# Windowed attention and a two-layer FFN: the opening reordered, and weight pieces with other engines' instructions

## The chip, the cores and the metric

The kernel runs on one core of a Trainium2 chip. The metric is the device time of one execution in microseconds, shown as the median of several runs. TensorE (PE) does the matrix products, VectorE (DVE), ScalarE (ACT) and GpSimd (POOL) work on tiles, SyncE (SP) issues DMAs. SBUF holds the tiles, PSUM the products.

## The reference

Attention over a window of 64 positions, for batch 8, 8 heads, 576 positions and head size 64, then an FFN over 4608 tokens, 512 to 2048 to 512, with a mish activation:

```python
scores = scale * np.matmul(q, k.transpose(0, 1, 3, 2))
mask = (rel >= 0) & (rel < window)          # window = 64
scores = np.where(mask, scores, -1000000000.0)
attn = softmax(scores)
x = (attn @ v) as [4608, 512]
h = x @ w_in
sp = np.where(h > 20.0, h, np.log1p(np.exp(np.minimum(h, 20.0))))
g = h * np.tanh(sp)
out = (g @ w_out).astype(np.float32)
```

The softmax divides by its sum + 1e-9. q, k and v are float32; w_in and w_out arrive as float64.

## The kernel before

**Tiling.** The 4608 tokens form 12 chunks of 384. A chunk's attention is done for four pairs of heads (p = 0 to 3), each giving 128 of the 512 channels of x. Its FFN has 16 steps f, each over 128 of the 2048 hidden channels. A float32 product is made of three products of rounded parts: x is kept as xh + xl, the weights as high and low parts, the activation g as gh + gl.

**Attention of a pair** (`att_scores`, `att_transpose`, `att_values`). TensorE makes the scores (L126) in two PSUM tiles; VectorE adds the mask and finds the extreme, in six pieces (L135, two records each); ScalarE takes the exponential and its sum (L138); VectorE makes the reciprocal (L140, L141); GpSimd multiplies, six pieces (L143). Chunks 0 and 1 transpose with TensorE (L162) and copy by ScalarE (L163). Later chunks transpose 32x32 blocks on VectorE (L152) and move the blocks by twelve DMAs from SyncE (L157). TensorE multiplies with v (L177), and ScalarE and VectorE split the result into xh and xl (L179, L180). Tiles pr and tr share the tag "pr" with two buffers.

**An FFN step** is twelve products into h_ps (L188, `ffn_in`), a chain over ScalarE and VectorE (L195 to L205), gh and gl on GpSimd (L206, L207), and nine products into three accumulators (L218, `ffn_out`), which follow two steps later (LAG). h_ps has two buffers. With `alone`, h is first copied to SBUF (L199), so that h_ps comes free early.

**Weights.** There are 32 pieces of 128x512 words of 64 bits (`load_w`), one for w_in and one for w_out of each f. The first five are loaded by SyncE, the rest by GpSimd's queue. Integer operations build the float32 value: L243 or L245 drops the sign, L246 clamps, L248 to L250 shift and join, L251 (ScalarE) rounds to the high part, L252 subtracts for the low part: on VectorE for pieces 6 to 25, on GpSimd for the others. Buffers: st three, wa four (tag "t", shared with the FFN's t).

**Order of the opening.** The attention of chunks 0 and 1 comes first, eight pairs one after the other, with eight weight pieces held back until named points. Then come 24 FFN steps, (1,0), (0,0), (1,1), (0,1) and so on, with two pieces each, which finish chunk 1 and half of chunk 0, with `alone`. Then chunk 0's steps 8 to 15 run, with chunk 2's attention between them, and from there every chunk's 16 steps with the next chunk's attention between them.

**What sets the order.** Each engine runs its instructions in one fixed order. It comes from the order of the code and from a scheduler that may move an instruction ahead of others on its engine. The PSUM banks: three tiles "acc" for a chunk's accumulators, two for h_ps, three "at" for attention and for the accumulators of chunk 1. In the first two chunks the even pairs' attention uses the "acc" banks.

Of the kernel before, what the change touches and what calls it, by code (L numbers as in the profile page):

```python
# [27 lines left out]
def tile_window_attn_mish_ffn(  # L28
# [83 lines left out]
    def att_scores(c, p, tiles):  # L112
        q_t, k_t = tiles

        if c < 2 and p % 2 == 0:
# [13 lines left out]
        for m in range(NM):  # L129
            first = [(c * NB + 2 * m + par) % blocks_per_seq == 0 for par in range(2)]  # L130
            mk = firsts[first.index(True)] if any(first) else mask
            for h in range(2):
# [2 lines left out]
                marks[c, p] = nc.vector.tensor_tensor_reduce(  # L135
# [5 lines left out]
        nc.vector.reciprocal(sm, sm)  # L141
        for j in range(HM):
            nc.gpsimd.tensor_scalar(pr[:, j, :], pr[:, j, :], sm[:, j:j + 1], 0.0, ALU.mult, ALU.add)  # L143
# [23 lines left out]
    def att_values(c, p, v_t, pT, x):
        xh, xl = x
        if c < 2 and p % 2 == 0:
            o_ps = ps_acc.tile([P, CH], F32, name="o_ps", tag="acc2")  # L170
        else:
            o_ps = ps_at.tile([P, CH], F32, name="o_ps", tag="at")
# [9 lines left out]
    def ffn_in(x, f, alone=False):  # L182
# [17 lines left out]
        nc.vector.tensor_scalar(t, t, EXP20, 1.0, ALU.min, ALU.add)  # L200
# [210 lines left out]
```

## Time and profile before

| | us |
|---|---|
| median of 3 runs (lowest, highest) | 1050.46 (1048.21, 1053.51) |
| the profiled execution | 1050.85 |
| its span in the profile | 1049.1 |
| TensorE busy | 963.9 (92%) |
| VectorE, ScalarE, GpSimd busy | 460.3, 600.4, 444.4 |
| TensorE waiting for gh (L206) | 23.6 |

A row of the timeline has the start and the length in us, the engine, line, operation, tiles written and read, the shape and a count (a matmul record counts twice where the product is taken in two passes); in brackets stands the idle time before it and what ended it. Lengths of neighbours overlap by under 0.1 us, so that the distance of two starts is the true cost of a busy engine. A row of the windows has the stretch, its length, then busy us and count for PE, weight loads, DVE, ACT and POOL, then TensorE's granted clock, the DMA share and GB/s. Rows of groups end with busy us, mean ns, and the idle time before. A row of the page on DMAs ends with KB of one and us from issue to landing.

### The profile page before, as it was taken

To read this page: it belongs to the slowest core of one execution; us is meant where nothing else is said; L and a number is where in the kernel's file an instruction comes from. 1 tells how busy PE (TensorE), PEld (TensorE's weight loads), DVE (VectorE), ACT (ScalarE), POOL (GpSimd) and SP (SyncE) were. 2 spreads that over 40 slices of the span, in tenths; PEclk is the share of its full clock that TensorE was granted. 3 is DMA by queue.
4 is the path that set the end of the run, shared out by engine and by line. 5 is a ranking of instruction groups with operands and counts; after the bars stand their busy time and mean duration, and the time that the engine had idled before them with its cause. 6 is when DMAs were issued, how large, how long until landed. Compare 5 with 4: busy or idle time off the path is not lost.

```text
span 1049.1 us, 18496 instructions
## 1 busy us (share of the span) xinstructions
PE 963.9 (92%) x6384; PEld 825.5 (79%) x6384; DVE 460.3 (44%) x1317; ACT 600.4 (57%) x1524; POOL 444.4 (42%) x729
## 2 busy tenths in 40 slices
PE   5577669996499999999999999999999999999997
PEld 4356558985388888888888888888888888888896
DVE  3679995333334334334343343344343443443232
ACT  4545666653356556565555565565665565655664
POOL 4445455342244344435344344444344444344332
PEclk9678999998599999999999999999999999999999
DMA  7544440013212222222222221221222221210000
GB/s 226 155 155 140 141 140 1 1 59 112 83 50 77 66 60 76 76 66 67 73 66 64 74 80 53 73 78 54 74 78 53 74 77 53 90 50 17 31 1 31
DMA packets 84957, 78.56 MB, mean 75 GB/s; under 512 B 11136, under 2 KB 76160, under 8 KB 84864
## 3 DMA queue, kind: packets, MB, share of 16 engines
q1 hardware_dynamic: 80976, 63.22, 20.4%
q0 software_dynamic: 3888, 14.16, 4.0%
q8 instruction: 51, 0.84, 0.3%
q14 instruction: 42, 0.34, 0.1%
HBM read 56.10 MB, written 9.44 MB: 62 GB/s over the span
## 4 chain that ended last, share of the span: by engine, by line
PE 81%; DVE 8%; DMA 3%; ACT 3%; issue 2%; SPq 2%; POOL 1%; ACTq 0%; DVEq 0%; POOLq 0%
PE h_ps L188 38%; PE acc L218 35%; PE o_ps L177 4%; PE s_ps L126 4%; DMA st<-w_out 1%; ACT pr L138 1%; DVE wa L249 1%; SPq L157 1%; DVE wa L250 1%; DVE wa L248 1%; DVE wa L246 1%; POOL pr L143 1%; DVE t L205 1%; DVE pr L135 1%; DVE tr L152 1%
## 5 line engine op out<-in xcount | busy, mean ns | idle before, releaser
L188 PE MATMUL h_ps<-xh,wi_h 128*128 128x384 f32 x768 | 267.5, 349 | 11.1 <-DVE t L205 5.1
L188 PE MATMUL h_ps<-xh,wi_l 128*128 128x384 f32 x768 | 265.3, 345 | 0.0
L188 PE MATMUL h_ps<-xl,wi_h 128*128 128x384 f32 x768 | 265.0, 345 | 0.0
L206 POOL TENSOR_SCALAR gh<-t 128x384 fp32r<-128x384 f32 x192 | 105.2, 548 | 373.4 <-DVE t L205 354.0
L218 PE MATMUL acc<-wo_h,gh 128*128 128x512 f32 x576 | 233.0, 404 | 23.6 <-POOL gh L206 23.6
L218 PE MATMUL acc<-wo_l,gh 128*128 128x512 f32 x576 | 231.2, 401 | 0.0
L207 POOL TENSOR_TENSOR gl<-t,gh 128x384 fp32r<-128x384 f32 x192 | 196.7, 1024 | 15.8
L218 PE MATMUL acc<-wo_h,gl 128*128 128x512 f32 x576 | 202.7, 396 | 0.0
L195 ACT ACTIVATE t<-h_ps 128x384 f32<-128x384 f32 x192 | 93.9, 489 | 188.5 <-PE h_ps L188 152.7
L200 DVE TENSOR_SCALAR t<-t 128x384 f32<-128x384 f32 x192 | 107.2, 558 | 161.9 <-ACT t L195 161.9
L188 PEld LDWEIGHTS h_ps<-xh,wi_h 128*128 128x128 f32 x768 | 147.0, 192 | 27.1 <-DVE t L205 7.4
L143 POOL TENSOR_SCALAR pr<-pr,sm 128x128 f32<-128x128 f32 x288 | 107.2, 391 | 144.0 <-DVE sm L141 130.3
L205 DVE SCALAR_TENSOR_TENSOR t<-t,h_ps 128x384 f32<-128x384 f32 x152 | 83.5, 549 | 185.8 <-ACT t L203 185.6
L138 ACT ACTIVATE pr<-pr,mx 128x128 f32<-128x128 f32 x288 | 111.8, 390 | 85.6 <-DVE mx L135 85.6
L201 ACT ACTIVATE t<-t 128x384 f32<-128x384 f32 x192 | 100.6, 524 | 99.0 <-DVE t L200 98.4
L188 PEld LDWEIGHTS h_ps<-xl,wi_h 128*128 128x128 f32 x768 | 147.3, 192 | 8.9
L188 PEld LDWEIGHTS h_ps<-xh,wi_l 128*128 128x128 f32 x768 | 147.2, 192 | 2.7 <-issue 2.1
L218 PEld LDWEIGHTS acc<-wo_h,gh 128*128 128x128 f32 x576 | 109.6, 190 | 47.6 <-POOL gh L206 27.9
L218 PEld LDWEIGHTS acc<-wo_h,gl 128*128 128x128 f32 x576 | 107.8, 187 | 25.1 <-issue 0.5
L218 PEld LDWEIGHTS acc<-wo_l,gh 128*128 128x128 f32 x576 | 109.6, 190 | 17.5
L202 ACT ACTIVATE t<-t,half_b 128x384 f32<-128x384 f32 x192 | 118.3, 616 | 5.3
L203 ACT ACTIVATE t<-t 128x384 f32<-128x384 f32 x192 | 100.6, 524 | 5.2
(47 smaller groups left out, 719.1 us busy)
## 6 DMA issues: line engine op xcount, KB each, us to landing
v_t<-vN SPq DMA_DIRECT2D x48, 384.0 KB, 3.5
pT<-tr SPq DMA_DIRECT2D x480, 24.0 KB, 1.8
k_t<-kT SPq DMA_DIRECT2D x47, 224.0 KB, 2.7
out<-o SPq DMA_DIRECT2D x36, 256.0 KB, 2.1
q_t<-qT SPq DMA_DIRECT2D x47, 192.0 KB, 2.4
st<-w_out POOLq DMA_DIRECT2D x14, 512.0 KB, 3.7
st<-w_in POOLq DMA_DIRECT2D x13, 512.0 KB, 3.8
st<-w_in SPq DMA_DIRECT2D x3, 512.0 KB, 6.4
```

Of the source, the lines that this page charges most:

```text
L138: nc.scalar.activation(pr[:, j, :], pr[:, j, :], AF.Exp, bias=mx[:, j:j + 1], scale=-1.0, accum_out=sm[:, j:j + 1])
L143: nc.gpsimd.tensor_scalar(pr[:, j, :], pr[:, j, :], sm[:, j:j + 1], 0.0, ALU.mult, ALU.add)
L188: nc.tensor.matmul(h_ps, w[:, f, cc, :], xx[:, cc, :], start=n == 0, stop=n == 3 * NC_ - 1)
L195: nc.scalar.activation(t, h_ps, AF.Exp)
L200: nc.vector.tensor_scalar(t, t, EXP20, 1.0, ALU.min, ALU.add)
L201: nc.scalar.activation(t, t, AF.Square)
L202: nc.scalar.activation(t, t, AF.Ln, bias=half_b, scale=0.5)
L203: nc.scalar.activation(t, t, AF.Exp, scale=-1.0)
L205: nc.vector.scalar_tensor_tensor(t, t, -1.0, h, ALU.add, ALU.mult)
L206: nc.gpsimd.tensor_scalar(gh, t, 1.0, 0.0, ALU.mult, ALU.add)
L207: nc.gpsimd.tensor_tensor(gl, t, gh.bitcast(F32), ALU.subtract)
L218: nc.tensor.matmul(acc[t], a[:, ts_], w[:, f, :], start=f == 0 and i == 0, stop=f == NF - 1 and i == 2)
```

## The change

**Order.** Chunk 0's attention stands alone at the start, with one weight piece after each pair's scores and three behind. Then come seven steps of chunk 0 (HEAD = 7) with chunk 1's attention between them, then chunk 0's steps 7 to 15 in turn with chunk 1's steps 0 to 8, then chunk 1's last seven steps with chunk 2's attention between them. Two pieces follow every step of chunk 0. All attention events stand in one list; loads of q, k and v run on from a chunk to the next.

**Banks.** Chunk 2's attention uses the three "acc" banks, which chunk 0 has left by then; chunk 1's uses "at".

**Weight pieces.** All are loaded by SyncE. L255 drops the sign on VectorE in every piece; the clamp and the last subtraction are on GpSimd in every piece (L256, L262).

**Attention.** Only chunk 0 transposes with TensorE, one of its two copies now on VectorE; chunk 1 takes the VectorE and DMA way. The six softmax pieces go by head. In chunk 0 sums and multiplies are taken per head, and four of six multiplies are on VectorE.

**FFN.** Only the last chunk copies h. The +1 moves from VectorE's min into Square's bias; in chunks 0 and 1 the min of odd steps is on GpSimd (L212).

```diff
+    def banks(c, p):
+        if c == 2 or (c == 0 and p % 2 == 0):
+            return [(ps_acc, "acc0"), (ps_acc, "acc1"), (ps_acc, "acc2")]
+        return [(ps_at, "at")] * 3
...
+            if c == 0:
+                nc.vector.tensor_scalar(sm[:, js], sm[:, js], 1e-9, None, ALU.add)
+                nc.vector.reciprocal(sm[:, js], sm[:, js])
+                for j in range(h * NM, (h + 1) * NM):
+                    if j % NM == 1:
+                        nc.gpsimd.tensor_scalar(pr[:, j, :], pr[:, j, :], sm[:, j:j + 1], 0.0, ALU.mult, ALU.add)
+                    else:
+                        nc.vector.tensor_scalar(pr[:, j, :], pr[:, j, :], sm[:, j:j + 1], None, ALU.mult)
...
-        if c >= 2:
+        if c > 0:
             tr = ap_.tile([P, P // 32, HM, 32], F32, name="tr", tag="pr", bufs=2)
...
-            nc.scalar.copy(pT[:, :, h * NM:(h + 1) * NM, :].rearrange("p r m i -> p m r i"),
-                           t_ps.rearrange("p m (r i) -> p m r i", i=32))
+            (nc.scalar.copy if h == 0 else nc.vector.tensor_copy)(
+                pT[:, :, h * NM:(h + 1) * NM, :].rearrange("p r m i -> p m r i"),
+                t_ps.rearrange("p m (r i) -> p m r i", i=32))
...
-        nc.vector.tensor_scalar(t, t, EXP20, 1.0, ALU.min, ALU.add)
-        nc.scalar.activation(t, t, AF.Square)
+        if c < 2 and f % 2:
+            nc.gpsimd.tensor_scalar(t, t, EXP20, 0.0, ALU.min, ALU.max)
+        else:
+            nc.vector.tensor_scalar(t, t, EXP20, None, ALU.min)
+        nc.scalar.activation(t, t, AF.Square, bias=one_b)
...
-        (nc.sync if i < 5 else nc.gpsimd).dma_start(st, src)
+        nc.sync.dma_start(st, src)
...
-        if 1 <= i < 14:
-            nc.vector.tensor_scalar(a, hi, 0x7FFFFFFF, None, ALU.bitwise_and)
-        else:
-            nc.scalar.activation(af, hi.bitcast(F32), AF.Abs)
-        nc.vector.tensor_scalar(af, af, BIG, TINY, ALU.min, ALU.max)
+        nc.vector.tensor_scalar(a, hi, 0x7FFFFFFF, None, ALU.bitwise_and)
+        nc.gpsimd.tensor_scalar(af, af, BIG, TINY, ALU.min, ALU.max)
...
-        (nc.gpsimd if i < 6 or i >= 26 else nc.vector).tensor_tensor(wl, af, wh.bitcast(F32), ALU.subtract)
+        nc.gpsimd.tensor_tensor(wl, af, wh.bitcast(F32), ALU.subtract)
...
-    both = [(1, f) for f in range(NF)]
-    for f in range(F2):
-        both.insert(2 * f + 1, (0, f))
-    segments = [(both, None, None), ([(0, f) for f in range(F2, NF)], 2, 1)]
...
+    HEAD = 7
+    steps = [(0, f) for f in range(HEAD)]
+    for f in range(HEAD, NF):
+        steps += [(0, f), (1, f - HEAD)]
+    third = 2 * len(steps) + 2
+    steps += [(1, f) for f in range(NF - HEAD, NF)]
+    starts = {c: 2 * len(steps) + 2 * NF * (c - 2) for c in range(2, NCHUNK)}
+    steps += [(c, f) for c in range(2, NCHUNK) for f in range(NF)]
...
+    atts[1].plan(0, 2 * HEAD / (NPAIR + 1))
+    atts[2].plan(third, (starts[2] - third) / (NPAIR + 1))
+    for c in range(3, NCHUNK):
+        atts[c].plan(starts[c - 1], (2 * NF - 2) / (NPAIR + 1))
```

What the order shows at three places.

VectorE in the middle of the opening, before (wa, st: a weight piece; wi_l, wo_l: its low part; t, h: the FFN step):

```order
L250 SCALAR_TENSOR_TENSOR wa_886<-st_884,wa_886 128x512
L205 SCALAR_TENSOR_TENSOR t_907<-t_907,h_911 128x384
L249 SCALAR_TENSOR_TENSOR wa_934<-st_932,wa_934 128x512
L246 TENSOR_SCALAR wa_944<-wa_944 128x512
L250 SCALAR_TENSOR_TENSOR wa_934<-st_932,wa_934 128x512
L252 TENSOR_TENSOR wo_l_105<-wa_886,wo_h_104 128x512
L248 TENSOR_SCALAR wa_944<-wa_944 128x512
L252 TENSOR_TENSOR wi_l_103<-wa_934,wi_h_102 128x512
```

The same engine in the change, at chunk 1's first steps:

```order
L255 TENSOR_SCALAR wa_1249<-st_1247 128x512
L255 TENSOR_SCALAR wa_1259<-st_1257 128x512
L214 TENSOR_SCALAR t_1194<-t_1194 128x384
L214 TENSOR_SCALAR t_1227<-t_1227 128x384
L258 TENSOR_SCALAR wa_1249<-wa_1249 128x512
L259 SCALAR_TENSOR_TENSOR wa_1249<-st_1247,wa_1249 128x512
L219 SCALAR_TENSOR_TENSOR t_1194<-t_1194,h_ps_1181 128x384
L260 SCALAR_TENSOR_TENSOR wa_1249<-st_1247,wa_1249 128x512
```

And GpSimd in the change, at the same place:

```order
L256 TENSOR_SCALAR wa_1249<-wa_1249 128x512
L256 TENSOR_SCALAR wa_1259<-wa_1259 128x512
L220 TENSOR_SCALAR gh_1195<-t_1194 128x384
L221 TENSOR_TENSOR gl_1196<-t_1194,gh_1195 128x384
L220 TENSOR_SCALAR gh_1228<-t_1227 128x384
L262 TENSOR_TENSOR wi_l_103<-wa_1249,wi_h_102 128x512
L221 TENSOR_TENSOR gl_1229<-t_1227,gh_1228 128x384
L262 TENSOR_TENSOR wo_l_105<-wa_1259,wo_h_104 128x512
```

The clamp and the subtraction have left VectorE's order; between L255 and L258 of a piece VectorE now waits for GpSimd.

TensorE in chunk 2's attention, before (s_ps: scores of the next pair; o_ps: values of the pair before, which need its DMAs into pT):

```order
L177 MATMUL o_ps<-pT_107,v_t 64x64 x2
L126 MATMUL s_ps<-k_t,q_t 64x128 x12
L177 MATMUL o_ps<-pT_107,v_t 64x64 x10
L188 MATMUL h_ps<-xh_1812,wi_h 128x384 x2
L188 MATMUL h_ps<-xl_1813,wi_h 128x384
L188 MATMUL h_ps<-xh_1812,wi_l 128x384
L188 MATMUL h_ps<-xl_1813,wi_h 128x384
L188 MATMUL h_ps<-xh_1812,wi_l 128x384
L177 MATMUL o_ps<-pT_106,v_t 64x64 x2
L126 MATMUL s_ps<-k_t,q_t 64x128 x12
```

And in the change, at the scores of pair 2:

```order
L234 MATMUL acc_1_1292<-wo_h,gl 128x512
L127 MATMUL s_ps<-k_t,q_t 64x128 x12
L234 MATMUL acc_2_1293<-wo_h,gh 128x512
L234 MATMUL acc_2_1293<-wo_l,gh 128x512
L188 MATMUL o_ps<-pT_106,v_t 64x64 x2
L234 MATMUL acc_2_1293<-wo_h,gl 128x512
L199 MATMUL h_ps<-xh_605,wi_h 128x384
```

The scores of pair 2 now stand ahead of the first values of the chunk, those of pair 0; before, each pair's scores stand behind the first two products of the pair before.

SyncE in the change, in chunk 1's attention (st: weights; pT: transposing DMAs):

```order
L249 DMA st_735<-w_in 128x512
L169 DMA pT0_106<-tr_591 32x192 x12
L104 DMA q_t_661<-qT 128x384
L106 DMA k_t_662<-kT 128x448
L249 DMA st_745<-w_out 128x512
L113 DMA v_t_622<-vN 128x6x128
L249 DMA st_846<-w_in 128x512
L249 DMA st_856<-w_out 128x512
L169 DMA pT1_107<-tr_721 32x192 x12
```

Before, no transposing DMA stands in the opening, and weights from the sixth piece on are not in this queue.

More of the change, by code (lines that the diff above doesn't have):

```diff
@@ L113, in att_scores @@
         q_t, k_t = tiles
-        if c < 2 and p % 2 == 0:
-            s_ps = [ps_acc.tile([P, NM, P], F32, name="s_ps", tag=f"acc{h}") for h in range(2)]
-        else:
-            s_ps = [ps_at.tile([P, NM, P], F32, name="s_ps", tag="at") for h in range(2)]
+        s_ps = [pool.tile([P, NM, P], F32, name="s_ps", tag=tag) for pool, tag in banks(c, p)[:2]]
         pr = ap_.tile([P, HM, P], F32, name="pr", bufs=2)
@@ L168, in att_values @@
         xh, xl = x
[L169 to L172, printed above, removed]
+        pool, tag = banks(c, p)[2]
+        o_ps = pool.tile([P, CH], F32, name="o_ps", tag=tag)
         for n in range(NB):
@@ L180, in att_values, with ffn_in @@
         nc.vector.tensor_tensor(xl[:, p, :], o_ps, xh[:, p, :].bitcast(F32), ALU.subtract)
-    def ffn_in(x, f, alone=False):
+    def ffn_in(c, x, f, alone=False):
         xh, xl = x
@@ L334, in flush @@
             ffn_store(c, accs.pop(c))
-    todo_w = [(w, f) for f in range(NF) for w in (load_w_in, load_w_out)]
+    todo_w = [(load_w_in, 0)]
+    for f in range(NF):
+        todo_w += [(load_w_in, f + 1)] * (f + 1 < NF) + [(load_w_out, f)]
     def take_w(n):
@@ L341, in take_w @@
             w(f)
-    xs = {}
-    first = [Att(c, c) for c in range(2)]
-    first[0].next = first[1]
-    ev = []
-    for u in range(2 * NPAIR):
-        a, p = first[u // NPAIR], u % NPAIR
-        ev += [(u, 2, a.scores, p), (u + 0.75, 1, a.transpose, p), (u + 1.25, 0, a.values, p)]
-    for _, _, fn, i in sorted(ev, key=lambda e: e[:2]):
-        fn(i)
-    xs[0], xs[1] = first[0].x, first[1].x
-    for u in (2, 4, 5, 5, 6, 7, 7, 7):
-        with tc.issue_after(marks[u // NPAIR, u % NPAIR].ins):
-            take_w(1)
@@ new lines, in tile_window_attn_mish_ffn @@
+    for f in range(HEAD, NF):
[4 more added lines that the diff above has]
+    steps += [(c, f) for c in range(2, NCHUNK) for f in range(NF)]
+    atts = [Att(c) for c in range(NCHUNK)]
+    for a, b in zip(atts, atts[1:]):
+        a.next = b
+    for p in range(2):
+        atts[0].load(p, "qk")
+        atts[0].load(p, "v")
+    ev = []
@@ L371, in tile_window_attn_mish_ffn @@
+    for n, (c, f) in enumerate(steps):
+        if f == 0:
+            while any(fn.__self__ is atts[c] for _, _, fn, _ in events):
+                run(events[0][0])
+        pend.append((c, f, ffn_in(c, atts[c].x, f, c == NCHUNK - 1)))
+        run(2 * n)
+        if len(pend) > LAG:
+            flush()
+        run(2 * n + 1)
+        if c == 0:
             take_w(2)
-        if att:
-            att.run(1e9)
     while pend:
```

99 lines of the change are left out of this document (40 added, 59 removed).

## The prediction

> **What bounds the kernel now.** I first read the page's slices, to see where TensorE is not busy, then windows of 25 us there, then the engines' timelines in those windows.
>
> ```profile
> span 1049.1 us, 18496 instructions
> PE   5577669996499999999999999999999999999997
> DVE  3679995333334334334343343344343443443232
> ```
>
> A slice is 26 us. From the seventh slice on TensorE is full but for the 10th and 11th (digits 6 and 4); what can be won lies there and in the first six slices.
>
> ```profile
> 75.00:100.00 25.00, 19.38 (x78) 16.41 (x79) 24.45 (x45) 13.27 (x27) 12.82 (x14) 0.86 0.36 113
> 125.00:150.00 25.00, 16.31 (x74) 13.54 (x73) 24.67 (x41) 16.70 (x31) 13.40 (x15) 0.97 0.49 164
> 175.00:200.00 25.00, 25.00 (x125) 22.40 (x124) 6.01 (x11) 13.30 (x27) 8.83 (x13) 1.00 0.00 1
> 250.00:275.00 25.00, 8.71 (x82) 6.76 (x82) 6.01 (x30) 5.69 (x26) 4.21 (x12) 0.56 0.40 120
> ```
>
> From 75 to 150 us VectorE (third figure) is busy 24.5 us of 25: the opening is bound by VectorE, which turns the weights' 64-bit words into two float parts. At 175 the weights are done and TensorE is full. At 250 nothing is busy: that is a wait, taken up below.
>
> **What VectorE really waits for.** Its busy time holds blocked time.
>
> ```profile
> 144.10 0.68 DVE L249 SCALAR_TENSOR_TENSOR wa<-st,wa 128x512 uint32<-128x512 uint32 x1
> 144.81 1.81 DVE L250 SCALAR_TENSOR_TENSOR wa<-st,wa 128x512 uint32<-128x512 uint32 x1
> 147.46 1.94 DVE L249 SCALAR_TENSOR_TENSOR wa<-st,wa 128x512 uint32<-128x512 uint32 x1
> ...
> 144.75 1.32 POOL L252 TENSOR_TENSOR wi_l<-wa,wi_h 128x512 fp32r<-128x512 f32 x1
> 147.56 1.28 POOL L252 TENSOR_TENSOR wo_l<-wa,wo_h 128x512 fp32r<-128x512 f32 x1
> ```
>
> The instruction that takes 0.68 us at 144.10 takes 1.81 and 1.94 us when GpSimd's 1.3 us subtraction runs beside it: it is lengthened by 1.13 and 1.26 us, nearly the subtraction's whole time. So work that leaves VectorE for GpSimd still holds VectorE up. How much of it, the rate tells:
>
> ```profile
> 78.73 0.69 DVE L250 SCALAR_TENSOR_TENSOR wa<-st,wa 128x512 uint32<-128x512 uint32 x1
> 102.95 0.35 DVE L200 TENSOR_SCALAR t<-t 128x384 f32<-128x384 f32 x1
> 103.22 0.42 DVE L246 TENSOR_SCALAR wa<-wa 128x512 f32<-128x512 f32 x1
> 103.56 0.68 DVE L250 SCALAR_TENSOR_TENSOR wa<-st,wa 128x512 uint32<-128x512 uint32 x1
> 104.16 0.42 DVE L248 TENSOR_SCALAR wa<-wa 128x512 uint32<-128x512 uint32 x1
> ...
> 119.67 0.55 DVE L205 SCALAR_TENSOR_TENSOR t<-t,h 128x384 f32<-128x384 f32 x1
> 120.14 0.69 DVE L252 TENSOR_TENSOR wo_l<-wa,wo_h 128x512 fp32r<-128x512 f32 x1
> ...
> 142.08 1.50 DVE L250 SCALAR_TENSOR_TENSOR wa<-st,wa 128x512 uint32<-128x512 uint32 x1
> ...
> 163.74 0.68 DVE L250 SCALAR_TENSOR_TENSOR wa<-st,wa 128x512 uint32<-128x512 uint32 x1
> ...
> 181.68 0.51 POOL L206 TENSOR_SCALAR gh<-t 128x384 fp32r<-128x384 f32 x1 [4.72 <-DVE t L205]
> 182.27 1.02 POOL L207 TENSOR_TENSOR gl<-t,gh 128x384 fp32r<-128x384 f32 x1
> ```
>
> From start to start, unblocked, VectorE needs 0.27 us for the 384-wide scalar op, 0.34 for a 512-wide one, 0.60 for a 512-wide two-input op, 0.47 for L205. L250 ends a piece. Between the rows at 78.73 and 142.08 lie 17 pieces and 9 FFN steps, 3.73 us a piece. VectorE's own work is 2x0.34 + 3x0.60 (+0.34 in a third of them, L243) = 2.6, and 9/17 x (0.27+0.47) = 0.4. The missing 0.73 x 17 = 12.4 us stand against 9 x (0.51+1.02) = 13.8 us of GpSimd: 90% of it shows as VectorE time. From 142.08 to 163.74 GpSimd does the subtraction, VectorE has four ops as in the changed kernel, and 5 pieces with two to three steps take 21.7 us: **4.33 us a piece, dearer than 3.73**.
>
> **The change, part by part.** (1) *Weight pieces.* All 32 now have four VectorE ops, 2x0.34 + 2x0.60 = 1.88 us, and on GpSimd a clamp and the 1.3 us subtraction. That is the form of the last five pieces plus the clamp. No row shows a 512-wide clamp on GpSimd; L206 gives 0.51 us at 384 columns, and L143 six ops of 128 in 2.11 us, 0.35 each:
>
> ```profile
> 252.91 2.11 POOL L143 TENSOR_SCALAR pr<-pr,sm 128x128 f32<-128x128 f32 x6 [7.42 <-DVE sm L141]
> 6.50 0.29 DVE L135 CUSTOM_DVE_ANT_0 pr<-s_ps,mask 128x128 f32<-128x128 f32 x1 [6.50 <-PE s_ps L126]
> 7.77 0.08 DVE L135 DVE_READ_ACCUMULATOR2_ANT mx<- 128x1 f32 x1
> 43.90 0.56 DVE L180 TENSOR_TENSOR xl<-o_ps,xh 128x384 fp32r<-128x384 f32 x1
> ...
> 70.91 0.69 PE L188 MATMUL h_ps<-xh,wi_h 128*128 128x384 f32 x1
> ```
>
> The line through both gives 0.6 us. Bounds of what it costs VectorE: 0 (hidden) and 0.8 (all of it, and two hand-overs between the engines); I take 0.4, nearer to the one-input gh, which blocks less than gl. A piece then costs 4.33 + 0.4 = 4.7 us with 0.45 steps in it, and a further step 1.9 us (0.14+0.47 on VectorE, the rest gh and gl at 90%).
>
> (2) *Stage A, chunk 0's attention alone.* VectorE has, up to the chunk's last xl, the ops of 7 pieces (14 us with the gaps between dependent ones), five sets of six reduces (1.3 us each by the rows at 6.50 and 7.77), and some 9 us of sums, reciprocals, half the multiplies, two-bank copies and xl: 29.5 us. GpSimd blocks it for seven clamps (2.8) and about four subtractions (5) and some multiplies (1). With the start at 6.5 us, x of chunk 0 is whole at **45 us**; now it is at 44.4 (the row at 43.90), but the FFN goes on to its first whole h_ps only at 70.91, after chunk 1's attention. Splitting each pair's multiplies over two engines shortens a chain of 2.1 us that VectorE's queue covers anyway: nothing.
>
> (3) *Stage B, eight steps of chunk 0 beside chunk 1's attention.* 14 pieces x 4.7 = 66; 8 steps where 6.3 are in that price, 3; three subtractions left from A, 4; four pairs at 3.7 us (1.3 reduces, 0.4 sums, 1.0 transposition, 0.5 xl, and a quarter of L143's 2.1), 15: **88 us**, to 133. TensorE needs 8 x 4.2 + 6 = 40 of it. SyncE now issues weights too, between the twelve transposing DMAs of a pair (7.9 us, row below); per pair that is about 11 us in 22, so it is hidden by VectorE; if VectorE took under 13 us a pair it would be bared.
>
> (4) *Stage C, both chunks in turn, until the last piece.* 11 x 4.7 + (10-5) x 1.9 = **61 us**, to 194. TensorE needs 42.
>
> (5) *The rest of the two chunks.* Unhindered, a step is 4.21 us:
>
> ```profile
> 195.05 2.09 PE acc L218 x9
> 197.14 2.12 PE h_ps L188 x12
> ```
>
> By TensorE's order nine groups of h_ps and ten of acc lie between the step of the last piece and the first scores of chunk 2; one of each should be done by then, as TensorE has slack: 8 x 2.12 + 9 x 2.09 = 36 us, to 230. At this point before (217.90) exactly as much FFN is left: five h_ps and seven acc groups.
>
> (6) *Chunk 2's attention.*
>
> ```profile
> 217.90 0.89 PE L126 MATMUL s_ps<-k_t,q_t 64*64 64x128 f32 x24
> 248.30 0.34 PE L177 MATMUL o_ps<-pT,v_t 128*64 128x64 f32 x4 [0.59 <-DMA pT<-tr]
> 248.56 0.89 PE L126 MATMUL s_ps<-k_t,q_t 64*64 64x128 f32 x24
> ...
> 274.98 0.48 PE L177 MATMUL o_ps<-pT,v_t 128*64 128x64 f32 x4 [5.97 <-DMA pT<-tr]
> ...
> 224.90 0.98 DVE L152 STREAM_TRANSPOSE tr<-pr 128x768 f32<-128x768 f32 x1 [2.01 <-POOL pr L143]
> 225.90 7.89 SPq L157 DMA_DIRECT2D pT<-tr  x12
> 282.25 1.13 ACT L195 ACTIVATE t<-h_ps 128x384 f32<-128x384 f32 x2 [1.74 <-PE h_ps L188]
> ...
> pT<-tr SPq DMA_DIRECT2D x480, 24.0 KB, 1.8
> ```
>
> Now each pair's scores stand behind the first o_ps of the pair before, which waits for its DMAs: 13.3 us a pair (248.30 to 274.98 are two), 64.4 us from 217.90 to the first whole h_ps of chunk 2 (282.25). In the new order the scores of pairs 1, 2 and 3 stand ahead of that, so softmax runs while the DMAs do. What is late next is the two buffers of tag pr: tr of a pair waits for the DMAs of the one before, 1.0 + 7.9 + 1.8 to land = 10.7 us. From scores to the first tr 7.0 (217.90 to 224.90), four times 10.7, then values, xh and h_ps 3: **53 us**, so chunk 2's first h_ps at 283. The freed banks themselves are never the last wait.
>
> (7) *From there* 1049.1 - 282.3 = 767 us with TensorE full and nothing moved. The min that lost its add keeps one VectorE op; Square takes the add at no row's cost. The ten later chunks are at nothing; if ScalarE's added bias operand cost 0.1 us it would still be hidden.
>
> **Sum**: 45 + 88 + 61 + 36 + 53 + 767 = 1050, against a span of 1049.1; the profiled execution took 1050.85 (1.75 around the span), 0.4 above the median of 1050.46. I forecast **1052 us**: opening gains paid back by GpSimd's blocking.
>
> The Trainium skill, page "SBUF — State Buffer", section "Who interferes with whom", says that the port pair shared by VectorE and GpSimd is an exclusive lock for a whole instruction. By it all of GpSimd's time, not 90%, counts against such VectorE ops, and 25 pieces would take some 5 us more: 1057, inside the forecast's own range. The trace agrees with a lock, at 90% (12.4 of 13.8 us).
>
> **Rivals.** *Ops that don't collide.* In the opening L205 now reads h from PSUM, not from a copy in SBUF.
>
> ```profile
> L205 DVE SCALAR_TENSOR_TENSOR t<-t,h 128x384 f32<-128x384 f32 x24 | 16.7, 697 | 16.7 <-ACT t L203 16.6
> L205 DVE SCALAR_TENSOR_TENSOR t<-t,h_ps 128x384 f32<-128x384 f32 x12 | 6.6, 547 | 12.0 <-ACT t L203 12.0
> ```
>
> The second form is never lengthened. If GpSimd works beside it, the reduces, xl and copies, and the clamp hides too, 18 x 0.47 + some 7 us of the rest + 25 x 0.4 = 26 us go: **1026**. The same page of the Trainium skill exempts a VectorE op with at most one SBUF input outside the two-port modes; 547 against 697 ns agrees. Against it: queues run in order, so VectorE seldom has such an op at the moment it is blocked.
>
> *Idle on top, slower.* A piece now goes VectorE, GpSimd, VectorE, and GpSimd's queue holds 2.1 us of L143 and 1.0 of gl ahead of clamps; in stage B the reduces of a pair wait for the pair before to land, 10.7 us after its transposition, with only 4 to 6 us of VectorE work in between. If each of 25 pieces waits 0.5 us more and each of four pairs 2 us, 20 us come on top: **1072**. It decides once VectorE stands idle over 10% of stages B and C.
>
> *Chunk 2's wait stays.* If the scores still run one pair at a time, 64 us instead of 53: **1063**. The order speaks against it.
>
> **Chances**: forecast 0.45 (its own range 1040 to 1062), no collision 0.28, idle 0.20, the wait stays 0.07. Range 1022 to 1077, the first and the last of these cases with the clamp's bounds. A measurement can tell about 0.5% (5 us): faster takes 0.28 and a quarter of the forecast's range, 0.38; slower 0.37; the same 0.25.
>
> **What would show it.** First h_ps of chunk 0 near 45 us; last L260 near 194; VectorE over 95% busy from 20 to 190 with L259 and L260 well above 0.8 us on average; chunk 2's first scores near 230 and first h_ps 53 us later; 767 us from there. A last L260 before 180 or after 205 makes the prediction wrong, and so would a last part other than 767.

## The result, and the profile after

The changed kernel takes **1020.83 us** (median of 4 runs, 1019.57 to 1021.59), the kernel before 1051.99 (4 runs, 1048.21 to 1054.14) on the same chip: ratio 0.971, with a 95% interval of 0.967 to 0.974. The profiled execution has a span of 1019.6 us against 1049.1. The forecast was 1052, with a range of 1022 to 1077: it was wrong, by 31 us at its centre.

The slices of the page of the changed kernel (span, TensorE and VectorE, 25.5 us each):

```profile
span 1019.6 us, 18461 instructions
PE   4677677998699999999999999999999999999998
DVE  5988767233333344444444444343344444444322
```

TensorE's low digits now lie in the first seven slices and in the 11th; the second dip of before (6 and 4, in the 10th and 11th) has become an 8 and a 6. VectorE's digits in the opening (second to seventh slice) are 6 to 9, lower than the forecast thought (over 95%).

The forecast named three places to look at. They stand in the timelines of VectorE (last weight piece), TensorE (first scores of chunk 2) and ScalarE (first whole h_ps of chunk 2); columns: start, duration, instruction.

```profile
178.72 1.39 DVE L260 SCALAR_TENSOR_TENSOR wa<-st,wa 128x512 uint32<-128x512 uint32 x1
213.82 0.89 PE L127 MATMUL s_ps<-k_t,q_t 64*64 64x128 f32 x24
267.88 1.13 ACT L206 ACTIVATE t<-h_ps 128x384 f32<-128x384 f32 x2 [1.74 <-PE h_ps L199]
```

The rows of before for the last two are at 217.90 and 282.25. So the gain of 29.5 us of span splits into 4.1 us up to chunk 2's scores, 10.3 in chunk 2's attention (54.1 us in place of 64.4), and **15.1 behind it** (751.7 in place of 766.8), in a part that the forecast held unmoved. Against the forecast, which already counted 11 us of gain in chunk 2's attention, the surprises are two: the opening is 16 us shorter than forecast, and the last part 15.

For the last part, the chain of waits in steady state, where TensorE is all of it (before: 2.12 us for twelve h_ps matmuls and 2.09 for nine acc matmuls, in the prediction's rows at 195.05 and 197.14). The changed kernel:

```profile
193.23 2.08 PE h_ps L199 x12
195.31 2.05 PE acc L234 x9
```

Each group is 0.04 us shorter, with nothing waited for, and the granted clock is 1.00 in both kernels, there and from 350 to 990 us. 160 steps of two such groups lie behind the first h_ps of chunk 2: 160 x 0.08 = 12.8 us of the 15 are a matter of the rate at which TensorE runs the same matmuls.

### The profile page after: what moved, and what is told of

Its sections match the earlier page's. It is cut to its first block, busy times and chain, and to the rows that moved or that the text cites. A ratio compares the mean times of both kernels' runs of the same rounds, so it can differ in the third digit from the quotient of the medians.

```text
span 1019.6 us, 18461 instructions
## 1 busy us (share of the span) xinstructions
PE 941.5 (92%) x6360; PEld 814.9 (80%) x6360; DVE 470.9 (46%) x1300; ACT 591.1 (58%) x1469; POOL 485.7 (48%) x755
## 4 chain that ended last, share of the span: by engine, by line
PE 78%; DVE 8%; SPq 4%; ACT 3%; POOL 3%; DMA 2%; issue 1%; DVEq 0%; ACTq 0%; POOLq 0%
PE h_ps L199 36%; PE acc L234 34%; PE o_ps L188 4%; SPq L169 3%; PE s_ps L127 3%; DVE wa L259 2%; DVE wa L260 2%; DVE wa L258 1%; DMA pT<-tr 1%; DMA st<-w_in 1%; POOL pr L155 1%; DVE wa L255 1%; ACT t L216 1%; DVE pr L137 1%; ACT pr L140 1%
## 5 line engine op out<-in xcount | busy, mean ns | idle before, releaser
L234 PE MATMUL acc<-wo_l,gh 128*128 128x512 f32 x576 | 228.9, 397 | 0.0
L234 PE MATMUL acc<-wo_h,gh 128*128 128x512 f32 x576 | 227.8, 396 | 0.4 <-POOL gh L220 0.4
L221 POOL TENSOR_TENSOR gl<-t,gh 128x384 fp32r<-128x384 f32 x192 | 198.7, 1036 | 14.6
L219 DVE SCALAR_TENSOR_TENSOR t<-t,h_ps 128x384 f32<-128x384 f32 x176 | 96.9, 551 | 227.7 <-ACT t L217 227.7
L234 PE MATMUL acc<-wo_h,gl 128*128 128x512 f32 x576 | 198.9, 393 | 0.7 <-POOL gl L221 0.7
L215 ACT ACTIVATE t<-t,one_b 128x384 f32<-128x384 f32 x192 | 118.1, 615 | 113.9 <-DVE t L214 100.1
L199 PEld LDWEIGHTS h_ps<-xl,wi_h 128*128 128x128 f32 x768 | 148.6, 193 | 10.3 <-DVE xl L191 2.4
L155 POOL TENSOR_SCALAR pr<-pr,sm 128x128 f32<-128x128 f32 x264 | 102.4, 407 | 112.2 <-DVE sm L153 59.8
L217 ACT ACTIVATE t<-t 128x384 f32<-128x384 f32 x192 | 100.4, 524 | 5.0
```

The source lines that it names most:

```text
L199: nc.tensor.matmul(h_ps, w[:, f, cc, :], xx[:, cc, :], start=n == 0, stop=n == 3 * NC_ - 1)
L215: nc.scalar.activation(t, t, AF.Square, bias=one_b)
L217: nc.scalar.activation(t, t, AF.Exp, scale=-1.0)
L219: nc.vector.scalar_tensor_tensor(t, t, -1.0, h, ALU.add, ALU.mult)
L221: nc.gpsimd.tensor_tensor(gl, t, gh.bitcast(F32), ALU.subtract)
L234: nc.tensor.matmul(acc[t], a[:, ts_], w[:, f, :], start=f == 0 and i == 0, stop=f == NF - 1 and i == 2)
```

## The experiments

All times below are medians; ratios are to the kernel before, run beside them. There it took 1051.4 to 1053.2 us, with single runs from 1048.2 to 1055.2, so that a difference of 2 or 3 us is little. The four columns on the right are read from each kernel's profile.

| kernel | us | ratio (95% interval) | last weight piece ends | chunk 2's scores | its first h_ps | from there |
|---|---|---|---|---|---|---|
| before | 1051.99 | 1 | 164.4 | 217.9 | 282.3 | 766.8 |
| changed | 1020.83 | 0.971 (0.967 to 0.974) | 180.1 | 213.8 | 267.9 | 751.7 |
| e1 before, 32 bytes on | 1040.14 | 0.989 (0.986 to 0.992) | 165.0 | 217.5 | 282.0 | 756.6 |
| e2 changed, 32 bytes back | 1034.06 | 0.983 (0.980 to 0.986) | 179.6 | 213.9 | 269.1 | 763.2 |
| e3 clamp on VectorE | 1031.07 | 0.980 (0.978 to 0.983) | 185.2 | 222.3 | 276.5 | 752.4 |
| e4 subtraction on VectorE | 1023.90 | 0.974 (0.971 to 0.976) | 180.8 | 214.5 | 269.7 | 752.2 |
| e5 copy of h | 1021.58 | 0.971 (0.969 to 0.974) | 180.3 | 215.3 | 269.3 | 751.2 |
| e6 chunk 2 not in freed banks | 1053.03 | 1.001 (1.000 to 1.003) | 181.0 | 240.8 | 301.6 | 752.0 |
| e9 before, new pieces | 1079.00 | 1.026 (1.023 to 1.028) | 194.7 | 246.4 | 310.5 | 766.3 |
| e10 no clamp | 1023.30 | 0.973 (0.970 to 0.977) | 176.9 | 214.5 | 268.7 | 752.6 |
| e11 loads by GpSimd | 1036.10 | 0.985 (0.982 to 0.988) | 196.3 | 230.0 | 283.3 | 751.3 |
| e12 before, new pieces, loads by SyncE | 1065.79 | 1.013 (1.010 to 1.016) | 176.4 | 232.7 | 297.1 | 765.7 |
| e16 e11 without clamp | 1030.32 | 0.980 (0.977 to 0.983) | 186.9 | 222.3 | 275.6 | 751.1 |
| e17 e11 and e2 together | 1047.76 | 0.996 (0.995 to 0.997) | 194.2 | 228.7 | 282.9 | 763.1 |
| e18 HEAD = 12 | 1010.02 | 0.960 (0.957 to 0.963) | 165.7 | 193.8 | 255.2 | 753.1 |

**The last part: where x, gh and gl lie.** The change adds a constant, one_b. It takes a slot of 32 bytes in SBUF, and everything allocated behind it moves by as much: x from byte 155808 of each partition to 155840, gh from 220000 to 220032 (counted on from x by the sizes of the tiles), gl and the tiles between likewise, while the weights stay. Two kernels put that to the test, one from each side: the kernel before with an unused constant, and the changed kernel with its two constants in one slot.

```diff
 # e1, on the kernel before
     nc.gpsimd.memset(half_b, 0.5)
+    pad = const.tile([P, 1], F32, name="pad")
+    nc.gpsimd.memset(pad, 1.0)
 # e2, on the changed kernel
-    half_b = const.tile([P, 1], F32, name="half_b")
+    both_b = const.tile([P, 2], F32, name="both_b")
+    half_b, one_b = both_b[:, 0:1], both_b[:, 1:2]
     nc.gpsimd.memset(half_b, 0.5)
-    one_b = const.tile([P, 1], F32, name="one_b")
     nc.gpsimd.memset(one_b, 1.0)
```

> The kernel before with one unused 4-byte constant behind half_b: every tile behind it (x, gh, gl, t and the rest) then starts 32 bytes higher, at the addresses of the changed kernel (xh0 at 155840, a multiple of 64, in place of 155808); the order is that of before. Placement theory (TensorE reads x or gh faster from a multiple of 64 bytes): a whole chunk takes 75.4 us in place of 77.0 between its output stores, the part behind chunk 2's first h_ps 752 in place of 767, and the time is about 1035 (ratio 0.985). Rival (the shorter matmul pitch comes from the changed softmax, min and Square, or from the order): 77.0 us a chunk and no change, 1051.

> The changed kernel with half_b and one_b as two columns of one tile, so that everything behind lies where it lay before (xh0 at 155808). Placement theory: 77.0 us a chunk, the last part 767, time about 1036. Rival (changed instructions): 75.45 us a chunk, 1021 as the changed kernel.

The chain of waits of e1:

```profile
193.02 2.08 PE h_ps L188 x12
195.10 2.05 PE acc L220 x9
```

The same view of e2:

```profile
192.94 2.12 PE h_ps L199 x12
195.06 2.09 PE acc L234 x9
```

The rate goes with the place, in both kernels. One unused constant makes the kernel before 1.1% faster; taking the 32 bytes back costs the changed kernel 13 us of its 31. What e1 does not get back is 4.9 us of its last part (756.6 against 751.7); TensorE's waits from 345 us on show some of it. Columns: what waited for what, us in total, times, longest. The kernel before:

```profile
PE h_ps L188 <- DVE t L205: 1.9, 4, 0.7
PE acc L218 <- POOL gh L206: 0.5, 1, 0.5
```

The changed kernel has only the second kind left, 0.4 us. The four waits stood at every second boundary of two chunks; they went with the new plan, which runs over the boundaries. That was not tried by itself.

Four more kernels ask which tile it is, and what place is a good one. e7 moves x back alone; e8, e13 and e14 add two, four and one more unused constants; e15 moves the two constants behind x, into a pool opened after that of x.

```diff
 # e7: half_b and one_b in one slot, as in e2, and behind x
+    pad = ap_.tile([P, 1], F32, name="pad", bufs=1)
+    nc.gpsimd.memset(pad, 1.0)
 # e14 (once), e8 (twice), e13 (four times; also mx bufs=2): behind one_b
+    pad0 = const.tile([P, 1], F32, name="pad0")
+    nc.gpsimd.memset(pad0, 1.0)
 # e15
+    late = ctx.enter_context(tc.tile_pool(name="late", bufs=1))
-    half_b = const.tile([P, 1], F32, name="half_b")
+    half_b = late.tile([P, 1], F32, name="half_b")
-    one_b = const.tile([P, 1], F32, name="one_b")
+    one_b = late.tile([P, 1], F32, name="one_b")
```

> The changed kernel with both constants in one tile (x starts 32 bytes past a multiple of 64, as before) and an unused 32 bytes behind x, so that gh and gl lie on multiples of 64 as in the changed kernel. If each operand's own place counts: h_ps matmuls at 175 to 177 ns from start to start as before, acc at 227 as in the changed kernel, a chunk 75.9 us. If x alone counts: both slow, 76.5 a chunk. If gh and gl alone count: both fast, 75.45.

> The changed kernel with two more unused constants, so that x starts at a multiple of 128 bytes and gh, gl at odd multiples of 64 (in the changed kernel it is the other way round). If 64 bytes are what counts: 75.45 us a chunk as in the changed kernel. If 128 count for x: below 75.2 a chunk with h_ps matmuls closer than 173 ns; for gh and gl: above 75.6.

> The changed kernel with four more unused constants (and two buffers of mx in place of three, for room): x at 155968, which is 64 past a multiple of 128 as in the changed kernel (155840) but 128 further on; gh and gl 96 past a multiple of 128 as in the kernel before. If places count modulo 128: h_ps matmuls 173 ns apart as in the changed kernel, acc 233 as before, a chunk about 76.1 us. If the period is longer: h_ps at 175 to 177 too and 76.5 us.

> The changed kernel with one more unused constant: x 96 past a multiple of 128, gh and gl 32 past. If only one place in 128 bytes is fast for each (64 for x, 0 for gh and gl): both slow, 76.5 us a chunk. If half of the 128 bytes is fast for x (64 to 127): h_ps 173 ns, a chunk 76.1 or less.

> The changed kernel with its two constants moved behind x: x at 155776, a multiple of 128; gh and gl where the changed kernel has them. If places count modulo 128 (0 was slow for x): h_ps at 175 to 177 ns, acc at 227, 75.9 us a chunk as with x 32 past. If x at 155904 was slow for another reason: 75.45.

The same rows of the chain, of e7 first and then of e13 and of e15:

```profile
192.51 2.12 PE h_ps L199 x12
194.63 2.04 PE acc L234 x9
```

```profile
193.99 2.08 PE h_ps L199 x12
196.07 2.09 PE acc L242 x9
```

```profile
192.08 2.10 PE h_ps L200 x12
194.19 2.08 PE acc L236 x9
```

| kernel | us | x: bytes past a multiple of 128 | gh, gl | twelve h_ps | nine acc | us a chunk |
|---|---|---|---|---|---|---|
| changed | 1020.83 | 64 | 0 | 2.08 | 2.05 | 75.45 |
| e13 | 1029.29 (one run) | 64 | 96 | 2.08 | 2.09 | 76.11 |
| e7 | 1025.96 (one run) | 32 | 0 | 2.12 | 2.04 | 75.87 |
| e2 | 1034.06 | 32 | 96 | 2.12 | 2.09 | 76.53 |
| e14 | 1032.05 (one run) | 96 | 32 | 2.12 | 2.09 | 76.47 |
| e8 | 1034.69 (one run) | 0 | 64 | 2.11 | 2.10 | 76.53 |
| e15 | 1027.58 (one run) | 0 | 0 | 2.10 | 2.08 | 76.16 |

x decides over h_ps, where it is streamed, and the tiles behind it over acc, where gh and gl are the loaded operand: e7 and e13 switch the one without the other. My first rule, a multiple of 64, fell with e8: x at a multiple of 128 is as slow as before. "64 past a multiple of 128" fits x in all rows. "A multiple of 128" fits gh and gl in all but e15, whose acc group is at 2.08 with gh and gl where the changed kernel has them. So the place modulo 128 is not the whole rule, and what in the chip it comes from is open.

**The opening: which queue issues the weight loads.** The forecast's price of a piece was read in the last five pieces of before. There GpSimd issued the loads of the weight words; in the changed kernel SyncE does. e11 gives them back to GpSimd; e16 leaves out the clamp besides, e10 the clamp alone; e17 is e11 with the places of e2.

```diff
 # e11
+    piece = itertools.count()
...
-        nc.sync.dma_start(st, src)
+        (nc.sync if next(piece) < 5 else nc.gpsimd).dma_start(st, src)
 # e10; and e16 on top of e11
-        nc.gpsimd.tensor_scalar(af, af, BIG, TINY, ALU.min, ALU.max)
```

> The changed kernel with the loads of the weight words from the sixth piece on issued by GpSimd, as before, and not by SyncE. Theory that this queue is what made pieces with clamp and subtraction on GpSimd dear (an issue takes 0.6 us there and waits for the buffer that VectorE has yet to free, with the next clamp behind it): 27 x (0.6 to 1.2) us, the last piece 15 to 30 us later, time 1036 to 1050. Rival (the queue costs nothing, GpSimd has a fifth idle): 1021 to 1025.

> The changed kernel without the clamp of the weight pieces (it only acts on values that these weights don't hold): the price of the clamp by itself. The prediction's 0.4 us a piece: the last weight piece 25 x 0.4 = 10 us earlier, chunk 2's first scores too, time 1011. Hidden on GpSimd (VectorE stands idle a fifth of the opening anyway): within 3 us of 1021. All of it on the path (0.7 us a piece and the hand-over): 1000.

> The changed kernel with the weight loads from the sixth piece on issued by GpSimd (e11_pool_queue, 1036 us) and without the clamp. If the prediction's 0.4 us a piece holds where GpSimd also issues the loads: the last piece 10 us before 196, time 1026. If the clamp is hidden there too: 1034 to 1036.

> The changed kernel with both causes taken back: weight loads from the sixth piece on issued by GpSimd, and the two constants in one tile so that x, gh and gl lie where they lay before. If these two are all that the forecast lacked: the last weight piece at 196, chunk 2's scores at 230, first h_ps at 283 to 284, 764 to 767 behind it, time 1049 (15 + 13 us above the changed kernel's 1021). If something else is in the gain: the two don't add, time under 1040.

With that one line back, the last piece ends at 196.3 and chunk 2's scores stand exactly where the forecast had them (230). Timelines of e11:

```profile
194.90 1.39 DVE L262 SCALAR_TENSOR_TENSOR wa<-st,wa 128x512 uint32<-128x512 uint32 x1
230.00 0.89 PE L127 MATMUL s_ps<-k_t,q_t 64*64 64x128 f32 x24
```

Its groups on GpSimd between 45 and 180 us (columns: operation, count, busy us and mean ns, then idle time of the engine just before them and what ended it) show the mechanism:

```profile
L251 POOL DMA_DIRECT2D st<-w_out x12 | 7.3, 605 | 15.4 <-DVE wa L262 10.7 <-DVE sm L152 3.8 <-PE h_ps L199 0.8
L251 POOL DMA_DIRECT2D st<-w_in x11 | 6.6, 601 | 4.9 <-DVE wa L262 4.9
```

23 issues take 13.9 us, and GpSimd stands 20.3 us ahead of them, 15.6 of it until VectorE's last operation on a piece (L262) has freed a buffer, with the clamps, multiplies, gh and gl of other work behind. SyncE has no work on tiles behind such a wait: in the changed kernel it stands some 90 us ahead of its weight loads (up to 215 us), and TensorE waits only 1.8 us for chunk 1's transposing DMAs, which share that queue (a row under e5). The loads themselves land no later in e11: 3.7 and 3.9 us after their issue (medians), as in the changed kernel. The groups on VectorE in the stage from x of chunk 1 to the last piece, of the changed kernel (127 to 180 us) and then of e11 (128 to 196), show where the time went:

```profile
L260 DVE SCALAR_TENSOR_TENSOR wa<-st,wa 128x512 uint32<-128x512 uint32 x9 | 8.8, 978 | 0.3
```

```profile
L262 DVE SCALAR_TENSOR_TENSOR wa<-st,wa 128x512 uint32<-128x512 uint32 x12 | 14.1, 1179 | 0.4
```

A piece costs about the same there (53 us for 9, 68 for 12, steps included); but the changed kernel has only 9 pieces left when chunk 1's attention is done, e11 still 12. The queue costs three pieces during that attention, when GpSimd also has its multiplies. By which of the waits between the engines GpSimd's standing reaches VectorE there was not taken apart.

The clamp shows how a price hangs on what is beside it. Under GpSimd's queue its removal brings the last piece 9.4 us earlier (196.3 to 186.9; expected 10, by the prediction's 0.4 us a piece), of which 7.7 are left at chunk 2's scores and 6 in the time (1030 in place of 1036; 1026 was expected). With SyncE issuing, its removal brings the last piece 3 us earlier, but chunk 2's scores not at all (214.5 against 213.8), and the time is 1023.3: the clamp is hidden.

e17 takes both causes back. Its three places:

```profile
192.81 1.39 DVE L262 SCALAR_TENSOR_TENSOR wa<-st,wa 128x512 uint32<-128x512 uint32 x1
228.66 0.89 PE L127 MATMUL s_ps<-k_t,q_t 64*64 64x128 f32 x24
282.85 1.13 ACT L206 ACTIVATE t<-h_ps 128x384 f32<-128x384 f32 x2 [1.74 <-PE h_ps L199]
```

Forecast 230, 283 and 767 from there; measured 228.7, 282.9 and 763.1, and 1047.8 us. The two causes add (15 and 13 us alone, 27 together), and with them back the changed kernel is 0.4% faster than before.

**The new pieces in the old order.** e9 puts the changed kernel's load_w body into the kernel before; e12 also lets SyncE issue all loads.

```diff
 # e9 and e12, on the kernel before
-        if 1 <= i < 14:
-            nc.vector.tensor_scalar(a, hi, 0x7FFFFFFF, None, ALU.bitwise_and)
-        else:
-            nc.scalar.activation(af, hi.bitcast(F32), AF.Abs)
-        nc.vector.tensor_scalar(af, af, BIG, TINY, ALU.min, ALU.max)
+        nc.vector.tensor_scalar(a, hi, 0x7FFFFFFF, None, ALU.bitwise_and)
+        nc.gpsimd.tensor_scalar(af, af, BIG, TINY, ALU.min, ALU.max)
...
-        (nc.gpsimd if i < 6 or i >= 26 else nc.vector).tensor_tensor(wl, af, wh.bitcast(F32), ALU.subtract)
+        nc.gpsimd.tensor_tensor(wl, af, wh.bitcast(F32), ALU.subtract)
 # e12
-        (nc.sync if i < 5 else nc.gpsimd).dma_start(st, src)
+        nc.sync.dma_start(st, src)
```

> The kernel before with the changed kernel's weight pieces alone: four VectorE operations in all 32 (the first always on VectorE), clamp and subtraction on GpSimd; the order and the places of before. The prediction's price (4.7 us a piece where VectorE is full, against 3.73): 17 pieces cost 16 us more, the last piece at 180, time 1067. If GpSimd's work is mostly hidden (a piece 3.3 us as in the changed kernel): the last piece at 157, and the time 1044 or, where chunk 2's attention takes the gain back, 1050.

> The kernel before with the changed weight pieces (as in e9_piece_form, 1079 us) and all loads of weight words issued by SyncE. Theory of the GpSimd queue: the last piece back from 195 to about 170, time 1055 or less. Rival (the pieces are dear because VectorE and GpSimd lengthen each other wherever VectorE is full): the last piece at 190 or later, time 1072 to 1079.

Alone, the new form is a loss: the last piece comes 30 us later than in before (twice the 16 expected) and the time is 27 us up. The queue gives back 13 of them (the last piece at 176.4, where about 170 was expected, and 1066 in place of 1055 or less); the other 14 stay. So neither theory is right alone, and what makes up the rest in the old order was not taken apart.

**Which engine a piece's work is on.** e3 has the clamp on VectorE again, e4 the subtraction of pieces 6 to 25.

```diff
 # e3
-        nc.gpsimd.tensor_scalar(af, af, BIG, TINY, ALU.min, ALU.max)
+        nc.vector.tensor_scalar(af, af, BIG, TINY, ALU.min, ALU.max)
 # e4
+    piece = itertools.count()
...
+        i = next(piece)
...
-        nc.gpsimd.tensor_tensor(wl, af, wh.bitcast(F32), ALU.subtract)
+        (nc.gpsimd if i < 6 or i >= 26 else nc.vector).tensor_tensor(wl, af, wh.bitcast(F32), ALU.subtract)
```

> The changed kernel with the clamp of the weight pieces back on VectorE (five VectorE operations a piece, no hand-over to GpSimd in the middle). Theory that VectorE's own time sets the opening (78% busy from 44 to 179 us, with the clamp hidden on GpSimd): 25 pieces x 0.34 us more, the last weight piece about 6 to 8 us later, time 1027. Theory that GpSimd's time is what holds VectorE up (clamp 0.72 us a piece there, at a lock of 90%, and 2.5 us of direct waits): the last piece 25 x (0.65 - 0.34) + 2.5 = 10 us earlier, time 1011. Both hidden by idle time of the queues: 1021.

> The changed kernel with the subtraction for the low weight part of pieces 6 to 25 back on VectorE, as it was before. Theory that VectorE's own time sets the opening: 20 pieces x 0.6 us = 12 us more, less the 1.0 us a piece by which L258 to L260 are lengthened beside it, 0.3 to 0.5 of it saved: time 1022 to 1028. Lock theory (the prediction's: GpSimd's 1.3 us subtraction costs VectorE 90% of its time, 1.2 us): 20 x 0.6 = 12 us less, time 1009.

Neither is faster, so the lock's price for the subtraction (12 us to be won in e4) is refuted for this kernel. e4 lies in the range that VectorE's own time gives (1022 to 1028), but its last piece comes only 0.7 us later, and 3 us of time are little. e3 costs 10 us, more than the 6 expected of its fifth operation. VectorE's waits in e3 from 45 to 185 us have one large row:

```profile
DVE xl L191 <- ACT xh L190: 10.5, 3, 9.2
```

One xl of chunk 1 came 9.2 us before its xh and held the queue: x of chunk 1 is whole at 136.7 in place of 126.7. That is the order that came out for this variant, so e3 does not price the clamp; e10 does.

**Operations that don't collide.** The rival at 1026 us rested on VectorE reading h from its bank.

```diff
 # e5, in ffn_in
+        if c < 2:
+            h = gl.bitcast(F32)
+            nc.scalar.copy(gl, h_ps)
```

> The changed kernel, but in the steps of chunks 0 and 1 ScalarE copies h out of its bank into the (still unused) gl tile, and VectorE's last operation of a step reads that copy (rounded to fp32r, so the values of these two chunks differ). With it VectorE's operation has two SBUF inputs again, as in the opening of before. Theory that the pieces came out cheaper than 4.7 us because this operation no longer collides with GpSimd: it is lengthened from 0.55 to about 1.0 us in 30 steps, the last piece comes some 8 us later (187) and the time is about 1029. Rival, that the bank is what is waited for (TensorE waits 34 us for it before h_ps): the copy frees it 2 to 3 us earlier a step, TensorE runs ahead, the last piece stays at 179 to 180 or comes earlier and the time is 1012 to 1018.

The groups on VectorE from 45 to 185 us, of e5 and then of the changed kernel:

```profile
L222 DVE SCALAR_TENSOR_TENSOR t<-t,gl 128x384 f32<-128x384 f32 x19 | 14.1, 744 | 10.3 <-ACT t L220 10.2
```

```profile
L219 DVE SCALAR_TENSOR_TENSOR t<-t,h_ps 128x384 f32<-128x384 f32 x19 | 10.4, 548 | 15.7 <-ACT t L217 15.7
```

The mean goes from 548 to 744 ns: the operation with two SBUF inputs is lengthened, though not to the expected 1.0 us, and the time is the same, 1021.6. TensorE's waits from 45 to 215 us say where the earlier release of the bank went, of the changed kernel and of e5:

```profile
PE h_ps L199 <- DVE t L219: 32.5, 9, 6.9
...
PE o_ps L188 <- DMA pT<-tr: 1.8, 3, 0.9
```

```profile
PE o_ps L188 <- DMA pT<-tr: 22.8, 5, 8.8
PE h_ps L199 <- ACT gl L209: 10.3, 9, 4.1
```

The wait for the bank falls from 32.5 to 10.3 us, and the one for chunk 1's transposed scores rises from 1.8 to 22.8: TensorE comes early to values that are not there yet. What VectorE loses does not show at its last piece (180.3 against 180.1). Neither theory's price is seen; since e5 changes two things at once, a small loss and a small gain that cancel are not excluded.

**Chunk 2's attention.** e6 keeps it off the banks that chunk 0 freed.

```diff
 # e6, in banks()
-        if c == 2 or (c == 0 and p % 2 == 0):
+        if (c == 0 and p % 2 == 0):
```

> The changed kernel with chunk 2's attention on the three banks that chunk 1 accumulates in, not on those that chunk 0 left. Theory (54 us in place of 64 from the first scores to the first h_ps comes from scores standing ahead of the values' wait in freed banks): 64 us again and 1031. Rival (it comes from the loads ahead, or from the new order of softmax): 54 us and 1021.

It costs 32 us, not 10. From first scores to first h_ps it takes 60.8 us in place of 54.1, but above all the scores start 27 us later, because chunk 1 holds the other three banks until its last step is stored. TensorE's timeline of e6:

```profile
240.81 1.20 PE L127 MATMUL s_ps<-k_t,q_t 64*64 64x128 f32 x24 [0.22 <-ACT o L241]
```

The wait is for ScalarE's copy of chunk 1's result (L241). In an order where chunk 1 ends last, the freed banks are a condition, not an improvement of 10 us. So e6 does not tell where the 10 us come from; VectorE's timeline of the changed kernel does, in the four transpositions of chunk 2's pairs:

```profile
221.34 0.97 DVE L164 STREAM_TRANSPOSE tr<-pr 128x768 f32<-128x768 f32 x1
232.11 0.98 DVE L164 STREAM_TRANSPOSE tr<-pr 128x768 f32<-128x768 f32 x1 [4.22 <-POOL gl L221]
242.76 0.98 DVE L164 STREAM_TRANSPOSE tr<-pr 128x768 f32<-128x768 f32 x1 [4.10 <-DMA pT<-tr]
253.73 0.98 DVE L164 STREAM_TRANSPOSE tr<-pr 128x768 f32<-128x768 f32 x1 [4.12 <-DMA pT<-tr]
```

They stand 10.7 to 11.0 us apart, the last two behind the DMAs of the pair before: the limit that the forecast put at 10.7 a pair, in place of 13.3.

**More of chunk 1 behind chunk 0.** The dip that is left is chunk 2's attention: 54 us, of which seven steps of chunk 1 cover 29.

```diff
 # e18
-    HEAD = 7
+    HEAD = 12
```

HEAD also sets over how many steps of chunk 0 chunk 1's attention is spread, so that it too has other slots.

> The changed kernel with chunk 1 trailing chunk 0 by twelve steps, not seven (HEAD = 12). Chunk 2's attention takes 54 us from its first scores to the first h_ps, and seven steps of chunk 1 cover 29 of them; twelve cover 50. Theory: five steps of chunk 1 (21 us) go from the opening, where TensorE has idle time, to behind chunk 0, so chunk 2's scores start up to 21 us earlier, at 193 to 200, first h_ps 54 us later at 247 to 254, time 1000 to 1007. Rival: chunk 0's last step is held by the last weight piece (180) and by VectorE, which then has the same pieces beside as many steps; scores stay near 205 or later and the attention between the steps gets longer: 1013 to 1021.

**1010.02 us**, ratio 0.960: 11 us below the changed kernel, the fastest of all. TensorE's slices, then its timeline and VectorE's and ScalarE's at the three places:

```profile
PE   4677648999899999999999999999999999999998
```

```profile
164.82 0.88 DVE L260 SCALAR_TENSOR_TENSOR wa<-st,wa 128x512 uint32<-128x512 uint32 x1
193.75 0.89 PE L127 MATMUL s_ps<-k_t,q_t 64*64 64x128 f32 x24
255.15 0.88 ACT L206 ACTIVATE t<-h_ps 128x384 f32<-128x384 f32 x2
```

With five fewer steps of chunk 1 beside them the last pieces come 14 us earlier, and the scores at 193.75, within the expected 193 to 200. The attention now takes 61.4 us, spread over more steps, so 12.7 of the 20 us gained at the scores are left at its end, and the time lies midway between the two theories' ranges. The dip has become an 8; the sixth slice, in the opening, has fallen from 7 to 4.

## Why the prediction was wrong

Its terms (us), beside the changed kernel and e17, the changed kernel with the two causes taken back:

| step | forecast | changed | e17 |
|---|---|---|---|
| A, x of chunk 0 whole | 45 | 46.2 | 47.5 |
| B, to x of chunk 1 | 88 | 80.5 | 78.8 |
| C, to the last piece | 61 | 53.4 | 67.9 |
| (5), to chunk 2's scores | 36 | 33.7 | 34.5 |
| (6), chunk 2's attention | 53 | 54.1 | 54.2 |
| (7), the last part | 767 | 751.7 | 763.1 |
| sum | 1050 | 1019.6 | 1046.0 |

- **Right**: A; (5), the count of what TensorE has left; and (6), with its reason, scores ahead of the values' wait and two pr buffers as the next limit.
- **Failed, first step: (7) "nothing moved".** 15 us. No matmul moved, but the tiles did: the added constant was costed as an operand of ScalarE, and not as a slot in SBUF. e2 puts 11.5 us of the 15 on that (763.2 in place of 751.7), and 1.2 ahead of it. Some 3.6 are left (763.2 against 766.8), of which the waits at the chunks' boundaries are 1.9.
- **Failed, second step: (3) "14 pieces x 4.7 = 66", the price of a piece carried over to the stage beside chunk 1's attention.** The opening is 16 us shorter than forecast, and e11 takes that back with one line. Stage B got through 16 pieces, not 14, in 80.5 us; by the forecast's own prices 16 pieces and 8 steps there make 16 x 4.7 + 0.8 x 1.9 + 4 + 15 = 96. In e11, with GpSimd issuing, the same sum for 13 pieces and 7 steps gives 82, and 79 were measured. In stage C the price held with either queue: 9 x 4.7 + 6 x 1.9 = 54 against 53.4 measured, and 67 against 68 in e11. So 4.7 was not too dear in itself. (3) counted the work that SyncE gets by the change, and left out what GpSimd is rid of: in e11 23 issues of 0.6 us and 20 us of standing before them. With the queue back (e17) the last piece, chunk 2's scores and its first h_ps come out to within 2 us of the forecast, and with the queue back the clamp is worth its 0.4 us. That agreement is of a sum: in e17 B was 9 us shorter than forecast, with 13 pieces, and C 7 us longer, with 12 in place of 11.
- **The test of VectorE over 95% busy** failed too: from 44 to 178.8 us it is busy 105 us of 135, in the windows of the changed kernel

```profile
44.00:178.80 134.80, 96.72 (x560) 81.82 (x557) 105.19 (x194) 63.97 (x150) 103.13 (x117) 0.85 0.40 127
```

  and GpSimd (last of the five busy figures) 103. The other half of that sign came true, L259 and L260 well above 0.8 us on average; VectorE's groups in the same stretch:

```profile
L259 DVE SCALAR_TENSOR_TENSOR wa<-st,wa 128x512 uint32<-128x512 uint32 x25 | 25.6, 1024 | 0.7
L260 DVE SCALAR_TENSOR_TENSOR wa<-st,wa 128x512 uint32<-128x512 uint32 x26 | 23.1, 887 | 0.6
```

  The lengthening is there, but the opening is a ring of queues in which no engine is full.
- **The rivals.** The one at 1026 came close to the time, but not by its reason: e5 gives VectorE's operation its second SBUF input back and the time stays, and with the operands where they lay before (e2), as this rival too had them, the time is 1034. Of its terms the hidden clamp came true (e10). "Idle on top, slower" was to decide once VectorE idles over 10%; it idles 22%, and the kernel is faster. Idle time of an engine was a wrong criterion where several queues wait for each other. "The wait stays" fell with the 54 us.
- **The lock.** The Trainium skill, page "SBUF — State Buffer", section "Who interferes with whom", says that a VectorE instruction with two SBUF inputs contends with a GpSimd instruction that reads SBUF. The durations agree (744 against 548 ns in e5). But the lock's price was taken as time on the path, and e4 shows that for the subtraction it isn't here.

## What to carry to other kernels

A price read in one stretch need not hold in another, where the engines have other work beside it: ask of every engine what the change takes from it, its DMA issues first, as well as what it adds. An engine that computes should not be the one that waits for buffers; here that was worth 15 us. And a new tile, however small, moves all tiles behind it: compare the start-to-start time of the same matmuls in both traces before explaining a gain by the change's intent, and try a pad of 32 bytes or two on a kernel that is bound by TensorE.

## What the runs showed of the hardware

TensorE's rate depends on where its SBUF operands start. Twelve 384-wide fp32r matmuls take 2.08 us with x at 64 bytes past a multiple of 128, and 2.10 to 2.12 at 0, 32 and 96; nine 512-wide ones take 2.04 to 2.10 with the place of the tiles behind x. That is 2 to 3% of a group, and 1.1 to 1.3% of the whole time here (e1, e2). The Trainium skill, page "SBUF — State Buffer", section "Operand start alignment", has as its rule that an operand starts at a multiple of its element size, and says that its runs timed nothing. All places here are multiples of 32 bytes, within that rule, and still differ in time.

An issue of a weight load takes 0.60 us on GpSimd (median in e11), and 0.33 to 0.56 on SyncE in the same kernel.
